# Rotated group order, sums of x beside the first expert, combinations on GpSimd and later stores in a fused sparse-attention and Sinkhorn-MoE kernel

## Chip, cores and metric

One core of a Trainium2 chip runs the whole program. The metric is device time in microseconds (us): the median over runs of the span that the device reports. TensorE does the matmuls (PE in the profile, PEld its weight loads), VectorE is DVE, ScalarE is ACT, GpSimd is POOL, and SyncE (SP) issues every DMA.

## The reference

```python
# attention: batch 4, heads 8, 576 positions, head size 64; masks local (32) or strided (32)
x = attention(q, k, v)                       # as rows: (2304, 512)
P = exp(x @ w_gate - max)                    # (2304, 8)
for _ in range(8):                           # Sinkhorn
    P /= P.sum(1, keepdims=True) + 1e-9
    P /= P.sum(0, keepdims=True) + 1e-9
    P *= N / E
out = 0
for e in range(8):                           # every expert, every row
    h = maximum(x @ w1[e], 0)                # 512 -> 1024
    out += P[:, e:e+1] * (h @ w2[e])         # 1024 -> 512
```

## The kernel before

Every matmul operand is split into a high and a low fp32r part, and a product is three matmuls (high times high, high times low, low times high).

**Attention and expert 0.** Attention comes first, then expert 0 runs in `slots`, each a `layer1` of one block of 128 hidden features for one chunk of rows and the `layer2` of the slot before it. The first half of the hidden features (36 slots, 256 rows each) runs beside the rest of the attention, the second half (20 slots, mostly 512 rows) beside gating and Sinkhorn. In the slots without attention work, Python generators are advanced a little per slot and so set the order of the instructions: `gating()`, and `build_s(p, k)`, which makes for row block p (of `NPASS` = 3, 768 rows each) and half k the four Strassen sums of x: it loads x from DRAM into the tile `sx`, adds two pairs on DVE (line 501), makes four sums on GpSimd (512), rounds them on ACT (518), subtracts on GpSimd (520) and stores the parts in DRAM (`sd`). Four of the six `build_s` run here, two beside pass 0.

**Experts 1 to 7.** Their work is cut into `NK` = 28 groups, an expert's quarter each (256 of the 1024 hidden features), and is done in three passes over blocks of 768 rows: `NG` = 84 groups. `step(g)` first ends the first layer of group g-1 (`finish_first`), then does the products of the first layer of g by Strassen's scheme (seven products of six matmuls each with 384 columns: 42 matmuls into the PSUM banks `ba`, `bb`, `bc`), then the second layer of g-1. In pass 0 the second layer is plain (`second`: 36 matmuls with 512 columns, line 676, each result added to `acc` on DVE, 683). In passes 1 and 2 it is Strassen's (`second_strassen`: 42 matmuls with 384 columns, 766, added to seven tiles `total` on DVE, 774), save in the last `LAST` = 2 groups of a pass, which are plain. After the last Strassen group of a pass, `combine` makes the result out of the seven totals (785: four operations on DVE, three on GpSimd, 128x768 each), and `turn` transposes it on TensorE and adds it to `acc` (794, 795), once per row tile, inside the loop of `second`.

**Weights.** In pass 0 `prep_w1` and `prep_w2` make the sums and the two parts of each group's weights out of the raw ones and store them in DRAM (`wd`, 598; `w2d`, 620); `w2_sums` forms its sums on DVE in two rows of `acc` (610 to 617). In passes 1 and 2 the same generators load them back (580, 632), group by group in the same order, into two buffers each (`g % 2`). The x operands of the next pass are loaded (`load_x`, 532 and 536) as the last group of a pass frees them one by one. `gated` multiplies by rows of the gate that `load_gate` broadcasts to all partitions (731), once per expert. In pass 0, after steps 4, 6, 8 and 10, `gate_rows` writes these rows (720, 721).

**Order.** All five engines work through their instructions in the order in which the program emits them; a wait at the head of a queue holds up all behind it. All DMAs are issued by SP, in order.

Of the kernel before, what the change touches and what calls it, by code (L numbers as in the profile page):

```python
# [55 lines left out]
def kernel(  # L56
# [429 lines left out]
    groups = [(p, e, j) for p in range(NPASS) for e in range(1, E) for j in range(FP)]  # L486
    NG = len(groups)
    wraw, w2raw, w2s, hg, yg, part = {}, {}, {}, {}, {}, {}

    def build_s(p, k):  # L490

        st = pools["sb"].tile([P, 4, 2, TN], F32, tag="sx", name=f"sx_{p}_{k}", bufs=1)
# [7 lines left out]
        for i in (0, 2):  # L500
            nc.vector.tensor_tensor(
                x[:, i : i + 2], x[:, i : i + 2], s[:, i : i + 2], op=ALU.add
            )
            yield
        x11, x21, x22, x12 = (x[:, i, :] for i in range(4))
        for i, (a, b, op) in enumerate((
            (x21, x22, ALU.add),
            (x21, x11, ALU.subtract),
            (s[:, 0, :], x11, ALU.subtract),
            (x12, s[:, 2, :], ALU.subtract),  # L510
        )):
            nc.gpsimd.tensor_tensor(s[:, i, :], a, b, op=op)
            if i % 2:
                yield
        yield
        for i in (0, 2):
            so = pools["sb"].tile([P, 2, 2, TN], F32R, tag="so", name=f"so_{p}_{k}_{i}", bufs=1)
            nc.scalar.activation(so[:, 0], s[:, i : i + 2], AF.Copy)
            yield
# [18 lines left out]
    def load_w1g(g):  # L538
        if g >= NK:
            return  # L540
        _, e, j = groups[g]
        if g == 0:
            t = raw_slots(4).rearrange("p (n i k f) -> p n i k f", n=4, i=2, k=2)
            wraw[g] = [t[:, i] for i in range(4)]
        elif g == 1:
            ts = [pools["hg"].tile([P, 2, TN], F32R, tag="hg", name=f"r_{g}_{i}") for i in range(4)]
            wraw[g] = [
                t.bitcast(F32).rearrange("p i t -> p (i t)")[:, : 4 * P]
                .rearrange("p (i k f) -> p i k f", i=2, k=2) for t in ts
            ]  # L550
# [15 lines left out]
    def load_w2g(g):  # L566
        if g >= NK:
            return
        _, e, j = groups[g]
# [4 lines left out]
    def prep_w1(g):  # L574
# [25 lines left out]

    w2o = [None, w2t.rearrange("p (b n) -> p b n", b=2)]
    w2sum = acc[:, HEAD : HEAD + 2, :].rearrange("p t d -> p (t d)")
    Q = 2 * P

    def w2_sums(g):

        src, w = w2raw.pop(g), w2o[g % 2]
        q = src.rearrange("p (n d) -> p n d", d=Q)
        t = w2sum.rearrange("p (n d) -> p n d", d=Q)
# [10 lines left out]
        nc.sync.dma_start(  # L620
            w2d[:, g, :].rearrange("p (b n) -> p b n", b=2), w.bitcast(F32)
        )
        yield

    def prep_w2(g):
        if g >= NG:
            return
        w = w2o[g % 2]
        if g >= NK:
            o = Q if strassen(g) else 0  # L630
            n = 8 * Q if strassen(g) else 4 * Q
            nc.sync.dma_start(
                w[:, :, o:n].bitcast(F32),
                w2d[:, g % NK, :].rearrange("p (b n) -> p b n", b=2)[:, :, o:n],
# [9 lines left out]
        if g:  # L644
            yield from w2_sums(g)
# [11 lines left out]
    LAST = 2  # L657

    def strassen(g):

        return NK <= g < NG and g % NK < NK - LAST

# [3 lines left out]
    def second(g, i, tag=None, parts=(0, 1)):  # L666

        p, e, j = groups[g]
# [17 lines left out]
        if ends(g):  # L686
            nc.sync.dma_start(out[t * P : (t + 1) * P, :], acc[:, i, :])

    def mul(g, wn, xn, bank, start):
        p, e, j = groups[g]  # L690
# [22 lines left out]
    gates, r11s = {}, {}  # L713
# [10 lines left out]
    def load_gate(p, e):  # L724
        if e == E:
            p, e = p + 1, 1
        if p == NPASS:
            return
        o = 2 * TN * (((E - 1) * (p - 1) + e - 1) % 2)
        t = raws[:, o : o + 2 * TN]  # L730
        nc.sync.dma_start(t, gd[e, 2 * TN * p : 2 * TN * (p + 1)].partition_broadcast(P))
        gates[p, e] = t.rearrange("p (h t) -> p h t", h=2)
# [6 lines left out]
    def gated(g, o, src, half):  # L739
        p, e, _ = groups[g]  # L740
        nc.vector.scalar_tensor_tensor(  # L741
            o, src[:, :TN], 0.0, gates[p, e][:, half, :], op0=ALU.max, op1=ALU.mult
# [33 lines left out]
    def combine():  # L776

        p1, p2, p3, p4, p5, p6, p7 = total
        for eng, o, a, b, op in (
            (nc.gpsimd, p2, p1, p2, ALU.add), (nc.vector, p6, p1, p6, ALU.add),  # L780
            (nc.vector, p7, p6, p7, ALU.add), (nc.vector, p6, p6, p5, ALU.add),
            (nc.vector, p3, p6, p3, ALU.add), (nc.gpsimd, p4, p7, p4, ALU.subtract),
            (nc.gpsimd, p5, p7, p5, ALU.add),
        ):
            eng.tensor_tensor(o, a, b, op=op)

    def turn(g, i):
# [7 lines left out]
        nc.vector.tensor_tensor(acc[:, i, :], y, acc[:, i, :], op=ALU.add)  # L795

# [31 lines left out]
    def step(g):  # L828
# [4 lines left out]
        if new:  # L833
            load_w1g(g + 2)
            if g >= NK:
                next(w2n, None)
                p, e, j = groups[g]
                if j == 1:
                    load_gate(p, e + 1)
# [26 lines left out]
        if new:  # L866
            mul(g, "t2", "s2", bb, True)
            plus(u2, bb, m1)
            next(w1n, None)
            mul(g, "t1", "s1", bc, True)  # L870
            next(w1n, None)
            next(w2n, None)
# [18 lines left out]
            if not strassen(g):  # L891
                relu_hi(g, 1, 1, u3)
        if not g:
            for x, only in rest:
# [6 lines left out]
        elif new:  # L901
            for i in range(6):
# [3 lines left out]
                if G >= NK and G % NK == NK - LAST:  # L906
                    turn(G, i)
                next(w1n, None)
                if i in (2, 4):
# [7 lines left out]
        for n in (w1n, w2n):  # L917
            for _ in n:
                pass
# [50 lines left out]
    def sums(*passes):  # L970
        for p in passes:
            for k in range(2):
                yield from build_s(p, k)

# [13 lines left out]
    def beside_second_half():  # L988

        work = {i: [] for i in range(20)}  # L990
        for g, i in enumerate((3, 12)):
            work[i].append(lambda g=g: load_w1g(g))
        for i, name in ((10, "x11"), (12, "s2"), (12, "s1"), (13, "x12")):
            work[i].append(lambda name=name: load_x(0, name))
        for g, s in enumerate((9, 15)):
            w = prep_w1(g)
            for i in range(5):
                work[s + i].append(lambda w=w: next(w, None))
        work[14].append(lambda: load_w2g(0))
        for i in range(6):  # L1000
            work[14 + i].append(lambda i=i: scale(0, i))
        return work

    slots = []
# [10 lines left out]
    for slot, (u, c, ft, last) in enumerate(slots):  # L1015
# [14 lines left out]
        if busy:  # L1030
            attention_rest()
            if at_k == NS + LAG:
                store_x()
                open_pools("right", ("sb", 1), ("hg", 8))
                gat, s0 = gating(), sums(0, 1)
                work = beside_second_half()
        else:
            next(gat, None)
            for _ in range(2):
                next(s0, None)  # L1040
# [3 lines left out]
    for x in (gat, s0):  # L1044
        assert next(x, x) is x
# [10 lines left out]
    s0 = sums(2)  # L1056
    for g in range(NG + 1):
        if g == NK:
            assert next(s0, s0) is s0
            open_pools("left", ("early", 2))  # L1060
        if g == NK + 1:
# [4 lines left out]
            ]  # L1066
        step(g)
        if g < NK:
            next(s0, None)
            if 4 <= g < 12 and g % 2 == 0:  # L1070
                gate_rows(g // 2 - 1)
            if g == NK - 1:
                load_gate(1, 1)
        p, n = divmod(g, NK)
        if 0 < p < NPASS:
            if n == 1:
                nc.sync.dma_start(
                    acc[:, :HEAD, :], yd[:, HEAD * (p - 1) : HEAD * p, :]
                )
            if 4 <= n < 4 + HEAD:  # L1080
                scale(p, n - 4)
# [81 lines left out]
```

## Time and profile before

| what | value |
|---|---|
| median of 3 runs | 1633.9 us (1633.17 to 6078.79) |
| profiled execution | 1634.83 us, its span 1633.0 us |
| PE busy | 1574.7 us, 96% |
| DVE / ACT / POOL busy | 1238.8 / 534.1 / 924.3 us |
| DMA | 426.26 MB, mean 261 GB/s |
| mean granted TensorE clock | 0.987 |

The span goes from the first to the last instruction. Matmuls are pipelined and the ends of their records are modelled, so starts are compared, not ends. A bracket at the end of a row of the timeline is the idle time of that engine ahead of the instruction and what ended it.

### The profile page before, as it was taken

To read this page: it belongs to the slowest core of one execution; us is meant where nothing else is said; L and a number is where in the kernel's file an instruction comes from. 1 tells how busy PE (TensorE), PEld (TensorE's weight loads), DVE (VectorE), ACT (ScalarE), POOL (GpSimd) and SP (SyncE) were. 2 spreads that over 40 slices of the span, in tenths; PEclk is the share of its full clock that TensorE was granted. 3 is DMA by queue.
4 is the path that set the end of the run, shared out by engine and by line. 5 is a ranking of instruction groups with operands and counts; after the bars stand their busy time and mean duration, and the time that the engine had idled before them with its cause. 6 is when DMAs were issued, how large, how long until landed. Compare 5 with 4: busy or idle time off the path is not lost.

```text
span 1633.0 us, 25381 instructions
## 1 busy us (share of the span) xinstructions
PE 1574.7 (96%) x9153; PEld 1467.9 (90%) x9153; DVE 1238.8 (76%) x2460; ACT 534.1 (33%) x1258; POOL 924.3 (57%) x880
## 2 busy tenths in 40 slices
PE   7999999989999999998999999999899999999997
PEld 5888778778888888887899999999899999999996
DVE  4665244389898989896488888888767888888886
ACT  6665222233434343432322222222223232222220
POOL 4221344146554656451577787777627778777781
PEclk9999999999999999999999999999999999999999
DMA  6553554697899789889966676666787666766661
GB/s 204 190 161 124 184 184 166 221 341 277 335 327 362 283 336 337 324 319 346 393 238 257 250 276 270 254 248 243 269 307 318 246 251 261 281 263 237 250 243 65
DMA packets 116700, 426.26 MB, mean 261 GB/s; under 512 B 9152, under 2 KB 62920, under 8 KB 101984
## 3 DMA queue, kind: packets, MB, share of 16 engines
q1 hardware_dynamic: 116576, 424.65, 69.5%
q8 instruction: 73, 1.20, 0.3%
q14 instruction: 51, 0.42, 0.1%
HBM read 287.72 MB, written 136.90 MB: 260 GB/s over the span
## 4 chain that ended last, share of the span: by engine, by line
PE 71%; DVE 16%; ACT 5%; DMA 4%; issue 2%; POOL 1%; SPq 0%; ACTq 0%; POOLq 0%; DVEq 0%
PE p L766 23%; PE bb L651 12%; PE ba L651 8%; PE bc L651 8%; PE yg L676 6%; PE y L429 5%; PE ph L405 5%; DVE acc L683 5%; DMA reg<-wd 2%; DVE acc L614 2%; DVE u L696 1%; ACT reg L180 1%; DMA sx<-xd 1%; DVE acc L613 1%; ACT h L704 1%
## 5 line engine op out<-in xcount | busy, mean ns | idle before, releaser
L774 DVE TENSOR_TENSOR total<-p,total 128x384 f32<-128x384 f32 x700 | 363.7, 557 | 0.0
L651 PE MATMUL bb<-reg 128*128 128x384 f32 x1512 | 310.4, 340 | 14.2 <-DVE u L696 8.9
L651 PEld LDWEIGHTS bb<-reg 128*128 128x128 f32 x1512 | 269.7, 190 | 19.3 <-DVE u L696 9.6
L651 PE MATMUL ba<-reg 128*128 128x384 f32 x1008 | 206.6, 340 | 11.3 <-ACT m L862 6.2
L651 PE MATMUL bc<-reg 128*128 128x384 f32 x1008 | 204.0, 336 | 6.8 <-ACT h L704 6.1
L651 PEld LDWEIGHTS ba<-reg 128*128 128x128 f32 x1008 | 181.6, 192 | 12.4 <-ACT m L862 6.5
L651 PEld LDWEIGHTS bc<-reg 128*128 128x128 f32 x1008 | 176.1, 188 | 13.0 <-ACT h L704 12.2
L696 DVE TENSOR_TENSOR u<-bb,m 128x384 f32<-128x384 f32 x168 | 93.2, 555 | 119.1 <-PE bb L651 117.4
L747 ACT ACTIVATE a<-u 128x384 fp32r<-128x384 f32 x104 | 54.7, 526 | 349.2 <-DVE u L741 349.0
L821 POOL TENSOR_TENSOR s1t<-m,u 128x384 f32<-128x384 f32 x52 | 52.9, 1016 | 187.5 <-DVE m L741 181.3
L683 DVE SCALAR_TENSOR_TENSOR acc<-yg,gate,acc 128x512 f32<-128x512 f32 x192 | 138.1, 743 | 12.6 <-PE yg L676 12.5
L429 PE MATMUL y<-w2t,h 128*128 128x512 f32 x432 | 112.3, 401 | 6.5 <-DVE h L412 5.6
L676 PE MATMUL yg<-w2t,h 128*128 128x512 f32 x504 | 117.7, 392 | 0.0
L676 PE MATMUL yg<-w2b,h 128*128 128x512 f32 x504 | 117.1, 390 | 0.0
L405 PE MATMUL ph<-reg,w 128*128 128x256 f32 (+1 forms) x672 | 114.3, 320 | 0.0
L676 PEld LDWEIGHTS yg<-w2t,h 128*128 128x128 f32 x504 | 95.0, 189 | 19.3
L766 PE MATMUL p<-s,w2t 128*128 128x384 f32 x624 | 112.3, 334 | 0.0
L766 PE MATMUL p<-s,w2b 128*128 128x384 f32 x624 | 112.3, 334 | 0.0
L676 PEld LDWEIGHTS yg<-w2b,h 128*128 128x128 f32 x504 | 94.4, 188 | 19.1
L766 PEld LDWEIGHTS p<-s,w2t 128*128 128x128 f32 x624 | 108.5, 188 | 0.0
L766 PEld LDWEIGHTS p<-s,w2b 128*128 128x128 f32 x624 | 108.5, 188 | 0.0
L751 POOL TENSOR_TENSOR a<-u,a 128x384 fp32r<-128x384 f32 x104 | 106.0, 1019 | 1.5 <-ACT a L747 1.5
(153 smaller groups left out, 2803.5 us busy)
## 6 DMA issues: line engine op xcount, KB each, us to landing
reg<-wd SPq DMA_DIRECT2D x56, 1792.0 KB, 10.0
wd<-reg SPq DMA_DIRECT2D x28, 1792.0 KB, 5.6
w2b<-w2d SPq DMA_DIRECT2D x26, 1792.0 KB, 6.8
w2t<-w2d SPq DMA_DIRECT2D x26, 1792.0 KB, 6.8
w2d<-w2b SPq DMA_DIRECT2D x14, 2048.0 KB, 7.6
w2d<-w2t SPq DMA_DIRECT2D x14, 2048.0 KB, 7.6
raws<-in_w SPq DMA_DIRECT2D x72, 256.0 KB, 4.8
sx<-xd SPq DMA_DIRECT2D x24, 384.0 KB, 5.6
```

Source lines behind the costliest of these rows:

```text
L405: nc.tensor.matmul(ph[:, :n], w[:, i, dt, :], xv(x, dt, c0, n), start=(k == 0), stop=(k == 3 * NDT - 1),)
L429: nc.tensor.matmul(y, h[:, a, i * P : (i + 1) * P], w[:, b, :], start=(ft == 0 and first), stop=(ft == FH - 1 and a == 1),)
L614: nc.vector.tensor_tensor(t[:, 3], t[:, 2], q[:, 3], op=ALU.subtract)
L651: nc.tensor.matmul(out[:, :TN], w[:, i, k, :], xops[x][:, xi, k, :], start=(start and n == 0), stop=(n == 5), skip_group_check=True,)
L676: nc.tensor.matmul(y, hg[g, i // 3, f][:, a, o : o + P], w[:, b, f, :], start=(f == 0 and a + b == 0), stop=(f == 1 and a == 1),)
L683: nc.vector.scalar_tensor_tensor(acc[:, i, :], y, gate[:, t, e : e + 1], acc[:, i, :], op0=ALU.mult, op1=ALU.add)
L696: nc.vector.tensor_tensor(o, bank[:, :TN], s, op=ALU.add)
L747: nc.scalar.activation(t[:, 0], src, AF.Copy)
L751: nc.gpsimd.tensor_tensor(t[:, 1], src, t[:, 0].bitcast(F32), op=ALU.subtract)
L766: nc.tensor.matmul(y[:, :TN], w[:, b, wi, d, :], h[:, a, :], start=(a + b == 0), stop=(a == 1),)
L774: nc.vector.tensor_tensor(o, y[:, :TN], o, op=ALU.add)
L821: nc.gpsimd.tensor_tensor(s1, m1, u3, op=ALU.add)
```

## The change

Groups carry a fourth number, their index k among the 28, and a pass begins with the two groups that the pass before ended with: pass 1 runs 26, 27, 0, ..., 25 and pass 2 runs 24, 25, 26, ..., 23. For these `KEEP` = 2 groups no weights are loaded. The store of the second-layer weights of groups 26 and 27 is put off until after steps 28 and 29. `LAST` becomes a tuple: pass 1 has one plain group at its end in place of two. The last part of `w2_sums` (617) and its store move from the end of a step into the next step, behind the second product; its sums get a tile of their own. In passes 1 and 2 the load of the second-layer weights is issued behind the products of a step, not at its head. All six `build_s` run beside expert 0, with two buffers for `sx` and a buffer for each `so`; their two additions go from DVE to GpSimd and their two subtractions from GpSimd to DVE. `combine` runs on GpSimd alone, and the six `turn`s stand behind the third to sixth block of `second`. The raw first-layer weights of group 1 use `raws`, those of the second layer of group 0 are loaded in the last slot instead of slot 14 of 20, and `acc` is loaded in six pieces.

```diff
-    groups = [(p, e, j) for p in range(NPASS) for e in range(1, E) for j in range(FP)]
+    KEEP = 2
+    groups = []
+    for p in range(NPASS):
+        for k in range(NK):
+            k = (k - KEEP * p) % NK
+            groups.append((p, 1 + k // FP, k % FP, k))
+    def kept(g):
+        return g >= NK and g % NK < KEEP
...
     def build_s(p, k):
-        st = pools["sb"].tile(..., tag="sx", bufs=1)
+        st = pools["sb"].tile(..., tag="sx", bufs=2)
...
-            nc.vector.tensor_tensor(
+            nc.gpsimd.tensor_tensor(
                 x[:, i : i + 2], x[:, i : i + 2], s[:, i : i + 2], op=ALU.add
             )
-            yield
...
+        for i, so in zip((0, 2), sos):
             nc.scalar.activation(so[:, 0], s[:, i : i + 2], AF.Copy)
-            yield
-            nc.gpsimd.tensor_tensor(
+        yield
+        for i, so in zip((0, 2), sos):
+            nc.vector.tensor_tensor(
                 so[:, 1], s[:, i : i + 2], so[:, 0].bitcast(F32), op=ALU.subtract
             )
...
     def prep_w1(g):
+        if kept(g):
+            return
         if g >= NK:
-            nc.sync.dma_start(whole, wd[:, g % NK, :])
+            nc.sync.dma_start(whole, wd[:, groups[g][3], :])
...
     def w2_sums(g):
+        w2sum = pools["hg"].tile([P, 2 * D], F32, tag="w2sum", bufs=1)
...
+        if g < NK - KEEP:
+            store()
+        else:
+            put_off.append(store)
...
     def prep_w2(g):
+        if kept(g):
+            return
...
-    LAST = 2
+    LAST = (NK, 1, 2)
+    def turning(g):
+        return g >= NK and g % NK == NK - LAST[groups[g][0]]
...
     def combine():
-        for eng, o, a, b, op in (
+        for o, a, b, op in (
+            (p6, p1, p6, ALU.add), (p7, p6, p7, ALU.add), (p6, p6, p5, ALU.add),
+            (p3, p6, p3, ALU.add), (p2, p1, p2, ALU.add), (p4, p7, p4, ALU.subtract),
+            (p5, p7, p5, ALU.add),
         ):
-            eng.tensor_tensor(o, a, b, op=op)
+            nc.gpsimd.tensor_tensor(o, a, b, op=op)
...
     def step(g):
-            if g >= NK:
-                next(w2n, None)
-        if g == 1:
-            for _ in w2_sums(0):
-                pass
...
             plus(u2, bb, m1)
+            for _ in w2_left.pop(G, ()):
+                pass
...
+        if g >= NK:
+            next(w2n, None)
         if not g:
+            for _ in range(3):
+                next(w2n, None)
             for x, only in rest:
                 layer2(*x, only)
...
-                if G >= NK and G % NK == NK - LAST:
-                    turn(G, i)
+                if turning(G):
+                    for x in ((), (), (0,), (1,), (2,), (3, 4, 5))[i]:
+                        turn(G, x)
...
+        if g < NK:
+            w2_left[g] = w2n
...
+    def beside():
+        for n in range(2 * NPASS):
+            w = build_s(*divmod(n, 2))
+            for i in (0, 3, 4, 5, 6):
+                at(3 * n + i - 4, next, w, None)
+        for g, i, s in ((0, 4, 9), (1, 14, 15)):
+            at(i, load_w1g, g)
...
+        at(19, load_w2g, 0)
```

## Rows read from the trace of the kernel before

**Rows 1.** The page, busy time of TensorE: us, share, instructions.
```profile
PE 1574.7 (96%) x9153; PEld 1467.9 (90%) x9153; DVE 1238.8 (76%) x2460; ACT 534.1 (33%) x1258; POOL 924.3 (57%) x880
```

**Rows 2.** Timeline of TensorE, starts of second layers: start, us, engine, line, operation.
```profile
334.40 8.36 PE L676 MATMUL yg<-w2b,h 128*128 128x512 f32 x36
...
752.94 8.36 PE L676 MATMUL yg<-w2b,h 128*128 128x512 f32 x36
...
776.33 9.02 PE L676 MATMUL yg<-w2t,h 128*128 128x512 f32 x36
...
798.24 2.07 PE L766 MATMUL p<-a,w2b 128*128 128x384 f32 x11
...
1163.02 2.25 PE L766 MATMUL p<-a,w2t 128*128 128x384 f32 x12
...
1204.81 4.28 PE L676 MATMUL yg<-w2t,a 128*128 128x512 f32 x18
...
1220.32 3.37 PE L766 MATMUL p<-a,w2b 128*128 128x384 f32 x18
...
1585.26 2.24 PE L766 MATMUL p<-a,w2t 128*128 128x384 f32 x12
...
1607.63 1.55 PE L676 MATMUL yg<-w2b,a 128*128 128x512 f32 x6
```

**Rows 3.** Waits from 150 to 320 us: us in total, times, longest.
```profile
DVE sx L501 <- DMA sx<-xd: 16.3, 5, 6.7
...
PE y L429 <- DVE h L412: 5.6, 2, 3.5
```

**Rows 4.** Timeline of TensorE beside gating, twice the same eight matmuls.
```profile
176.46 3.61 PE L339 MATMUL pl<-reg,wgs 128*128 128x512 f32 x8
...
186.29 2.00 PE L339 MATMUL pl<-reg,wgs 128*128 128x512 f32 x8
```

**Rows 5.** The tile sx, GpSimd's sums: ns min/median/max.
```profile
L512 POOL TENSOR_TENSOR sx<-sx x24: 995/1017/1209, 175.9 to 554.7; 128x384 f32<-128x384 f32 x24
```

**Rows 6.** Timeline of step 1.
```profile
323.30 1.21 PE L651 MATMUL bc<-reg 128*128 128x384 f32 x6
...
327.59 0.69 DVE L610 TENSOR_TENSOR acc<-raws 128x512 f32<-128x512 f32 x1 [4.46 <-DMA yd<-acc]
...
330.72 2.29 PE L651 MATMUL ba<-reg 128*128 128x384 f32 x6 [6.21 <-ACT m L862]
```

**Rows 7.** Timeline of a late step of pass 0.
```profile
715.48 1.26 DVE L617 TENSOR_TENSOR w2b<-acc,w2b 128x1024 fp32r<-128x1024 f32 x1
...
718.48 1.28 PE L651 MATMUL bc<-reg 128*128 128x384 f32 x6
...
721.67 0.56 DVE L708 SCALAR_TENSOR_TENSOR h<-ba,h 128x384 fp32r<-128x384 f32 x1 [1.71 <-ACT h L704]
```

**Rows 8.** Line 614, DVE: ns min/median/max.
```profile
L614 DVE TENSOR_TENSOR acc<-acc,raws x28: 424/1396/1953, 328.8 to 759.1; 128x256 f32<-128x256 f32 x28
```

**Rows 9.** The chain that ended last, between passes 0 and 1: start, us, what.
```profile
751.05 14.41 DMA reg<-wd
768.01 23.26 DMA reg<-wd
```

**Rows 10.** Stretch 750 to 800: busy us of each engine, granted clock, DMA share, GB/s.
```profile
750.00:800.00 50.00, 40.97 (x185) 36.47 (x185) 25.63 (x40) 8.92 (x18) 11.42 (x12) 0.90 1.01 400
```

**Rows 11.** Timeline between passes 1 and 2.
```profile
1166.63 1.30 PE L766 MATMUL p<-a,w2t 128*128 128x384 f32 x6 [1.37 <-DVE total L774]
...
1175.84 5.41 DVE L785 TENSOR_TENSOR total<-total,total 128x768 f32<-128x768 f32 x4
...
1181.77 2.29 PE L651 MATMUL bb<-reg 128*128 128x384 f32 x6 [4.48 <-DVE u L696]
```

**Rows 12.** Line 785, GpSimd's part of combine: ns min/median/max.
```profile
L785 POOL TENSOR_TENSOR total<-total,total x6: 1846/2520/2573, 1168.9 to 1602.6; 128x768 f32<-128x768 f32 x6
```

**Rows 13.** Line 632, loads of second-layer weights, all 56.
```profile
DMA to landing us min/median/max: 4.8/6.8/12.4
```

More of the change, by code (lines that the diff above doesn't have):

```diff
@@ L540, in load_w1g @@
             return
-        _, e, j = groups[g]
-        if g == 0:
+        _, e, j, _ = groups[g]
+        if g < 2:
             t = raw_slots(4).rearrange("p (n i k f) -> p n i k f", n=4, i=2, k=2)
             wraw[g] = [t[:, i] for i in range(4)]
[L545 to L550, printed above, removed]
         else:
@@ L643, in prep_w2 @@
         yield
-        if g:
-            yield from w2_sums(g)
+        yield from w2_sums(g)
     def product(w, x, out, start):
@@ L685, in second, with store_out @@
         )
-        if ends(g):
-            nc.sync.dma_start(out[t * P : (t + 1) * P, :], acc[:, i, :])
+        if ends(g) and not turning(g):
+            store_out(p, i)
+    def store_out(p, i):
+        t = 6 * p + i
+        nc.sync.dma_start(out[t * P : (t + 1) * P, :], acc[:, i, :])
     def mul(g, wn, xn, bank, start):
-        p, e, j = groups[g]
+        p = groups[g][0]
         product(wops[g % 2][:, :, W_AT[wn]], xn, bank, start)
@@ L722, in gate_rows, with load_gate @@
         nc.sync.dma_start(gd[:, 4 * P * c : 4 * P * c + n * P], lt[:E, : n * P])
[L724 to L727, printed above, removed]
+    spans = []
+    for g in range(NK, NG):
+        if strassen(g) and (not strassen(g - 1) or groups[g][1] != groups[g - 1][1]):
+            spans.append(g)
+    def load_gate(n):
+        if n == len(spans):
             return
-        o = 2 * TN * (((E - 1) * (p - 1) + e - 1) % 2)
+        p, e, _, _ = groups[spans[n]]
+        o = 2 * TN * (n % 2)
         t = raws[:, o : o + 2 * TN]
         nc.sync.dma_start(t, gd[e, 2 * TN * p : 2 * TN * (p + 1)].partition_broadcast(P))
-        gates[p, e] = t.rearrange("p (h t) -> p h t", h=2)
+        gates[spans[n]] = t.rearrange("p (h t) -> p h t", h=2)
     def form_tile(g, name):
@@ L795, in turn @@
         nc.vector.tensor_tensor(acc[:, i, :], y, acc[:, i, :], op=ALU.add)
+        if ends(g):
+            store_out(groups[g][0], i)
     def finish_first(g, s):
@@ L916, in step @@
                 second(G, i)
-        for n in (w1n, w2n):
-            for _ in n:
-                pass
+        for _ in w1n:
+            pass
+        if g < NK:
+            w2_left[g] = w2n
+        else:
+            next(w2n, None)
     LAG = 3
@@ L968 @@
         )
[L970 to L973, printed above, removed]
     def open_pools(side, *names):
@@ L1033 @@
                 store_x()
-                open_pools("right", ("sb", 1), ("hg", 8))
-                gat, s0 = gating(), sums(0, 1)
-                work = beside_second_half()
+                open_pools("right", ("sb", 1))
+                gat, work = gating(), beside()
         else:
             next(gat, None)
-            for _ in range(2):
-                next(s0, None)
             for x in work.get(slot - len(slots) + 20, ()):
@@ L1043 @@
         prev = (u, c, ft, last)
-    for x in (gat, s0):
-        assert next(x, x) is x
+    assert next(gat, gat) is gat
     for name in ("s3", "x22", "s4"):
@@ L1066 @@
             ]
+        if g == NK - 1:
+            load_gate(0)
         step(g)
         if g < NK:
-            next(s0, None)
             if 4 <= g < 12 and g % 2 == 0:
                 gate_rows(g // 2 - 1)
-            if g == NK - 1:
-                load_gate(1, 1)
+        elif g < NK + KEEP:
+            for store in put_off[g - NK :: KEEP]:
+                store()
         p, n = divmod(g, NK)
         if 0 < p < NPASS:
[L1076 to L1081, printed above, removed]
+            i = n - 3
+            if 0 <= i < HEAD:
+                nc.sync.dma_start(acc[:, i, :], yd[:, HEAD * (p - 1) + i, :])
+            if 0 <= i - 2 < HEAD:
+                scale(p, i - 2)
     for x in stacks.values():
```

74 lines of the change are left out of this document (34 added, 40 removed).

## Prediction

> **What bounds the kernel now.** I read the page first: TensorE is busy for 96% of the span [rows 1], so only two things can give time, fewer columns or fewer holes. Then the timeline of TensorE alone, where the reader is to compare starts of second layers. Between 798.24 and 1163.02 there are 25 steps of passes 1 and 2, 14.59 us each; nothing but TensorE sets them, so 84 matmuls of 384 columns take 0.174 us apiece. A plain step without disturbance takes 15.51 us (1204.81 to 1220.32), which leaves (15.51 - 42 x 0.174) / 36 = 0.228 us for a matmul of 512 columns [rows 2]. With these two paces every other interval shows its holes:
> - pass 0, 334.40 to 752.94: 26 steps, 418.5 us, 16.10 each, so 15.3 us more than 26 x 15.51;
> - pass 0 to 1, 752.94 to 798.24: 45.3 us for two plain steps, 14.3 too many;
> - pass 1 to 2, 1163.02 to 1220.32: 57.3 us for one Strassen step and two plain ones (45.6), 11.7 too many;
> - the end, 1585.26 to 1607.63: 22.4 us for a Strassen step, 7.8 too many [rows 2].
>
> The views of waits and of the timeline then say what makes each hole; they are cited where I use them. The stretches without holes, some 730 us of passes 1 and 2, can't get faster.
>
> **The change part by part.** The sum is made against the profiled execution, whose span is 1633.0 us with 1.8 us around it (1634.8); the median of the runs is 0.9 us below that, so the same saving is taken off 1633.9.
>
> *A. Sums of x beside expert 0.* DVE waits 16.3 us for the loads of `sx`, because its addition stands at the head of its queue, and the rectifying operation that TensorE needs (412) stands behind it: TensorE waits 5.6 us for that [rows 3]. After the longer wait it also runs at the lower of its two clocks: the same eight matmuls take 3.61 us instead of 2.00 [rows 4]. Together 7.2 us. The additions go to GpSimd, on which TensorE waits for nothing here, so these holes go. New are two more `build_s`: on GpSimd each is two additions of 128x768 (1.85 us, the least of that size [rows 12]) and four sums of 1.02 [rows 5], 7.8 us; it comes once in three slots of 24 x 0.228 = 5.5 us, so GpSimd has 16.4 us for 7.8, and the weight splits fit in the rest. What can wait on it is ACT: its rounding of the sums stands ahead of the next rectification. It is emitted a slot later, the loads three slots earlier, and a rectification has nearly a slot of slack, so I take 0.5 us lost (0 to 3). **Gain 6.7 (4 to 9).** The upper end is above 7.2, since the clock is also low for what stands around those eight matmuls.
>
> *B. Step 1.* DVE waits 4.46 us for the DMA that empties the two rows of `acc` which `w2_sums` borrows; ACT's copy of m stands behind ACT's rounding of these sums, and TensorE waits 6.21 us [rows 6]. After 323.30 three products (18 matmuls, 3.1 us) were left, so the second layer could begin at 326.4 instead of 334.40 [rows 2, 6]: a hole of 8.0. With a tile of its own nothing waits for that DMA. In its place the sums of group 0 run in step 0, ahead of the additions of expert 0's last `layer2` on DVE: one operation of 1024 (1.26 [rows 7]), two of 256 (0.42 [rows 8]) and one of 512 (0.8 as an estimate, twice a 256), 2.9 us, part of it while DVE has nothing else. What is late next is the PSUM bank of the third product of step 1, by 1.3 us (0 to 2.9). **Gain 6.7 (5 to 8).**
>
> *C. The steps of pass 0.* Two causes. First, two `build_s` stand in these steps and crowd DVE and GpSimd; they go. Second, at the end of a step DVE does line 617 (1.26 us, after a wait for ACT) ahead of the operations that free a PSUM bank, and the third product starts late for it [rows 7]. The change moves 617 behind the addition of the second product, where DVE now sits idle for 1.71 us [rows 7], so it costs nothing if it fits, and its store passes SP later, behind the loads of raw weights instead of ahead of them. The cover is thin: an operation of DVE on two SBUF tiles beside GpSimd takes longer, 1.40 us in the median against 0.42 at the least for the same shape [rows 8], so 617 may take 2.2 us and spill 0.5 us. The spill delays the middle of the step, while its end has become 1.26 us emptier; I take 0.1 us a step (0 to 0.5), 2.6 in all. The four `gate_rows` stay; I leave their steps the mean excess of 0.6, 2.4 in all. 15.3 - 2.6 - 2.4: **gain 10.3 (5 to 13).**
>
> *D. Pass 0 to pass 1.* The chain goes through two loads of `wd` that take 14.41 and 23.26 us [rows 9], and between 750 and 800 us the DMA engines are full at 400 GB/s, 20 MB in all [rows 10]. Kept groups take away two loads of `wd` and two of `w2d` (1792 KB each from the code, 7.3 MB), and two stores of 2048 KB (4.2 MB) move behind steps 28 and 29. Some 8.5 MB stay, 5.5 of them x: seven loads of 768 KB, each with about a step from its issue to its use. At 400 GB/s the first five need 9.8 us, and the one asked for last of these is wanted some 12 us later. Residue 0.8 us (0 to 6). **Gain 13.5 (8 to 14.3).**
>
> *E. Pass 1 to pass 2.* In place of three steps with two plain ones come two Strassen steps and a plain one. The wait of 1.37 us behind the two low parts stays [rows 11]. The wait of 4.48 us goes: DVE is held for 5.41 us by `combine` while the product's bank waits for it [rows 11]. On GpSimd seven operations take 1.85 to 2.57 us each [rows 12], 13 to 18 us. Counted from the start of the last Strassen second layer, the fourth total is there at about 7 us, so the two results that the first three turns need at 7 + 5 x (1.85 to 2.57) = 16.3 to 19.9; TensorE comes to the first turn at 14.59 + 1.37 + 3 x 1.37 = 20.1. The other two are there at 20 to 25, and wanted at 25.7 with some 0.5 for each turn. Both just fit, and nothing else on GpSimd is in a hurry there. New: beside a GpSimd that never pauses, two operations of `finish_first` on two SBUF tiles (708) can each wait for the rest of one of its operations, 0 to 3.7 us together; the product's bank stands behind them. I take 2. The turns: of the 41.8 us from 1163.02 to 1204.81 [rows 2], 14.59 + 1.37 + 4.48 + 15.51 are named, 5.8 left for turns and low clock; the transposes alone, at a quarter of 0.228, are 1.4. I take 3. After: 14.59 + 15.96 + 15.51 + 3 + 2 = 51.1 against 57.3. **Gain 6.2 (3 to 8).**
>
> *F. The end.* The same `combine` before the last plain step: 22.4 becomes 14.59 + 1.37 + 2 = 18.0. **Gain 4.4 (2.5 to 6.4).** The turns stay.
>
> *Nothing:* the loads of `acc` in six pieces (steps 31 to 36; they are used 20 steps later), `load_gate` (a step ahead), the raw weights of group 1 (in `raws`, which the split of group 0 has left by then).
>
> The Trainium skill, page "SBUF — State Buffer", section "Who interferes with whom", says that a VectorE instruction with two SBUF inputs and a GpSimd instruction that reads SBUF exclude one another, and the later one is blocked until the other ends. It speaks against putting more on GpSimd beside such operations; by it alone, with every 617 and both 708s blocked for a whole operation, C would be about 5 and E and F 4.5 and 2.7, and the time 1595. The trace agrees that the same operation takes from 0.42 to 1.95 us [rows 8].
>
> **Sum.** 6.7 + 6.7 + 10.3 + 13.5 + 6.2 + 4.4 = 47.8 us, 1633.9 - 47.8 = **1586 us**. The low ends together give 27.5 (1606), the high ends 58.7 (1575).
>
> **Rivals.**
> 1. *DVE becomes the pace of pass 0.* If 617 is blocked in its new place, a step stays near 15.8 to 15.9 and C gives 3 instead of 10: 1594. For it: the spread of line 614 [rows 8]. Against: the end of the step loses the same 1.26 us.
> 2. *The transition stays with the DMA.* If the loads of x are the late ones, most of the 14.3 stays: 1599. For it: the engines at 400 GB/s [rows 10]. Against: more than half of these bytes go.
> 3. *GpSimd crowds expert 0.* If ACT waits 3 us for each of six sums, 18 us of A's gain turn round: 1604. Against: 7.8 us of work in 16.4.
> 4. *Slower: second-layer weights arrive late.* Their load is now issued behind the products, 42 x 0.174 = 7.3 us later, in 52 steps of passes 1 and 2, and must land within 14.59 us. Above that each microsecond costs 52; from 15.5 us on all of the gain is gone, at 16 us the time is 1633.9 - 48 + 73 = 1659. For it: it now follows directly on the load of `wd`, which took up to 23.26 us [rows 9]. Against: the 56 loads of this kind land after 4.8 to 12.4, 6.8 in the median [rows 13].
>
> That the change doesn't do what it says would be a kept group that waits for its buffer all the same, which is rival 2.
>
> **Chances and range.** Forecast 0.74, rival 1 0.12, rival 2 0.06, rival 3 0.05, rival 4 0.03. What a measurement tells from no change is about 2%, 33 us, so 1601. The forecast, rival 1 and half of rivals 2 and 3 lie below: faster 0.89, within 2% 0.08, slower 0.03. The range takes in the high ends and rivals 1 and 2: 1575 to 1604.
>
> **What would show it.** Right: no wait of TensorE for 412 beside expert 0; second layers of pass 0 15.5 to 15.6 us apart; none of 20 us or more at the two transitions; the first turn without a wait; 85% or more of the steps of passes 1 and 2 still at 14.59. Wrong: TensorE waits for `w2b` or `w2t` in passes 1 and 2, ACT waiting for `sx` beside expert 0, or steps of pass 0 above 15.8.

## The result, and the profile after

The changed kernel takes 1596.2 us (median) against 1633.5 us for the kernel before on the same chip: ratio 0.9773, 95% interval 0.9751 to 0.9795. One run of each kernel (2188.5 and 6078.8 us) fell in a much slower state; the medians take it in and the ratio leaves it out. The profiled execution has a span of 1594.2 us, 38.8 less than before; the forecast took off 47.8. The page, busy time of each engine, answers to [rows 1]:

```profile
PE 1558.7 (98%) x9159; PEld 1461.1 (92%) x9159; DVE 1273.4 (80%) x2460; ACT 539.5 (34%) x1261; POOL 972.9 (61%) x899
```

Of the 38.8 us, 16.0 were busy time of TensorE and 22.8 its idle time. As before, the starts of second layers on TensorE's timeline tell where the time went; they answer to [rows 2]. The first two rows are the gate's first product and the first step's first product, which bound the stretch beside expert 0.

```profile
162.92 2.00 PE L339 MATMUL pl<-reg,wgs 128*128 128x512 f32 x8
...
313.72 1.22 PE L667 MATMUL ba<-reg 128*128 128x384 f32 x6
...
335.00 8.37 PE L696 MATMUL yg<-w2b,h 128*128 128x512 f32 x36
...
739.68 8.36 PE L696 MATMUL yg<-w2b,h 128*128 128x512 f32 x36
...
755.22 8.36 PE L696 MATMUL yg<-w2t,h 128*128 128x512 f32 x36
...
770.76 3.35 PE L794 MATMUL p<-a,w2b 128*128 128x384 f32 x18
...
1135.91 3.28 PE L794 MATMUL p<-a,w2t 128*128 128x384 f32 x18
...
1150.48 2.24 PE L794 MATMUL p<-a,w2b 128*128 128x384 f32 x12
...
1168.22 4.29 PE L696 MATMUL yg<-w2t,a 128*128 128x512 f32 x18
...
1186.65 3.59 PE L794 MATMUL p<-a,w2b 128*128 128x384 f32 x18
...
1551.18 2.25 PE L794 MATMUL p<-a,w2t 128*128 128x384 f32 x12
...
1568.92 4.29 PE L696 MATMUL yg<-w2b,a 128*128 128x512 f32 x18
```

Set against the same marks of the kernel before (its gate began at 163.85, its step 0 at 307.41), each part has its measured gain. E runs over three steps on either side, from 1135.91 in the changed kernel:

| part | before | after | gain | forecast |
|---|---|---|---|---|
| A, gate to step 0 | 143.6 | 150.8 | **-7.2** | 6.7 (4 to 9) |
| B, step 0 to its second layer | 27.0 | 21.3 | 5.7 | 6.7 (5 to 8) |
| C, 26 steps of pass 0 | 418.5 | 404.7 | 13.9 | 10.3 (5 to 13) |
| D, pass 0 to 1 | 45.3 | 31.1 | 14.2 | 13.5 (8 to 14.3) |
| E, pass 1 to 2 | 57.3 | 50.7 | 6.6 | 6.2 (3 to 8) |
| F, the end | 22.4 | 17.7 | 4.6 | 4.4 (2.5 to 6.4) |

These sum to 37.8; 0.9 more came ahead of the gate. Five terms came out near their size, and A has the wrong sign: without it the sum is 45.0 against the 41.1 forecast for those five. So the question for the experiments was what happens beside expert 0.

The view of waits of the changed kernel, TensorE's over the whole run (us in total, times, longest), names little there:

```profile
PE y L429 <- DVE tail L442: 6.9, 1, 6.9
PE pc L376 <- DVE g L373: 4.8, 2, 3.7
...
PE p L794 <- DVE total L802: 2.8, 2, 1.4
PE bb L667 <- DVE u L720: 2.5, 2, 1.3
...
PE bb L667 <- DMA reg<-sd: 1.6, 1, 1.6
```

The two waits of [rows 3] for the sums are gone. In their place stand one of 6.9 us at 300 us and two of 1.1 and 3.7 us at 248 and 256 us. The windows show what comes with them (us, busy of each engine, granted clock, DMA share, GB/s):

```profile
240.00:270.00 30.00, 24.81 (x123) 21.04 (x122) 25.12 (x43) 6.27 (x12) 19.36 (x15) 0.89 0.61 199
270.00:290.00 20.00, 20.00 (x88) 16.09 (x87) 6.55 (x6) 4.29 (x7) 13.35 (x11) 1.00 1.03 391
290.00:310.00 20.00, 13.09 (x48) 10.35 (x47) 7.51 (x9) 7.68 (x13) 7.71 (x7) 0.83 0.62 226
```

In the first and third TensorE stands idle for 5.2 and 6.9 us, 12.1 in all between the two marks, and the granted clock falls to 0.89 and 0.83 of 2.4 GHz. The kernel before was idle for 7.2 us between the same marks and had one stretch at a lower clock (0.91, from 160 to 200 us). Of the 7.2 us that A lost, 4.9 are thus more idle time. The other 2.3 are the same matmuls taking longer, as the lower clock makes them: behind the wait at 300 us twelve of them take 5.33 us instead of 2.88.

**The hole at 300 us** is read backwards on the timeline (start, us, engine, line, operation, wait and releaser):

```profile
277.30 1.33 SPq L542 DMA_DIRECT2D reg<-sd  x2
278.68 2.70 SPq L534 DMA_DIRECT2D sd<-so  x2
281.48 0.60 SPq L546 DMA_DIRECT2D reg<-xd  x1
282.12 4.46 SPq L534 DMA_DIRECT2D sd<-so  x2
286.64 5.59 SPq L565 DMA_DIRECT2D raws<-in_w  x4
...
292.54 0.85 ACT L527 ACTIVATE so<-sx 128x768 fp32r<-128x768 f32 x1 [9.32 <-DMA sd<-so]
296.45 0.84 ACT L527 ACTIVATE so<-sx 128x768 fp32r<-128x768 f32 x1 [3.06 <-DMA sd<-so]
...
297.62 1.27 POOL L592 TENSOR_TENSOR raws<-raws 128x512 f32<-128x512 f32 x1 [11.72 <-DMA raws<-in_w]
...
298.94 0.69 DVE L412 SCALAR_TENSOR_TENSOR h<-ph,h 128x512 fp32r<-128x512 f32 x1 [15.00 <-ACT h L411]
...
299.55 2.48 DVE L442 TENSOR_TENSOR tail<-y,tail 128x512 f32<-128x512 f32 x4
```

TensorE's own timeline has the wait:

```profile
300.38 5.33 PE L429 MATMUL y<-w2t,h 128*128 128x512 f32 x12 [6.91 <-DVE tail L442]
```

ACT's last two roundings write into `so`, whose stores of the sums before were issued behind 768 KB loads of x operands; with the DMA engines full (1.03, 391 GB/s) the four stores issued there each take 12.7 us to land, against 2.7 in the median of all 24. Behind the roundings stands ACT's copy of `h`, behind that DVE's rectification (line 412, [rows 3]'s victim too), behind that in DVE's queue the addition 442, which frees the bank that TensorE waits for.

**The waits at 248 and 256 us** lie in the short slots of 256 rows, where the gate's chain on DVE (lines 368 to 380) must pass between two products. Timeline of DVE and GpSimd there and in a slot before it:

```profile
227.30 1.85 POOL L510 TENSOR_TENSOR sx<-sx 128x768 f32<-128x768 f32 x1 [2.12 <-DMA sx<-xd]
227.72 1.45 DVE L369 TENSOR_SCALAR g<-g 128x18 f32<-128x18 f32 x1
...
242.78 1.84 POOL L510 TENSOR_TENSOR sx<-sx 128x768 f32<-128x768 f32 x1 [8.56 <-DMA sx<-xd]
243.27 1.52 DVE L380 SCALAR_TENSOR_TENSOR gate<-gate,r 128x144 f32<-128x144 f32 x1
...
245.66 1.83 POOL L510 TENSOR_TENSOR sx<-sx 128x768 f32<-128x768 f32 x1 [1.04 <-DMA sx<-xd]
245.67 1.99 DVE L371 TENSOR_TENSOR gate<-gate,g 128x144 f32<-128x144 f32 x1
...
252.45 1.25 DVE L380 SCALAR_TENSOR_TENSOR gate<-gate,r 128x144 f32<-128x144 f32 x1
...
255.81 0.60 PE L376 MATMUL pc<-g,ones 128*128 128x8 f32 x2 [3.72 <-DVE g L373]
```

Each of the three DVE operations at 227, 243 and 245 us, 0.2 to 0.3 us by itself, ends 0.02 to 0.17 us after the GpSimd addition beside which it began (229.17 and 229.15, 244.79 and 244.62, 247.66 and 247.49). The Trainium skill, page "SBUF — State Buffer", section "Who interferes with whom", says that the two engines share a port pair that one instruction holds whole; these ends agree with it. Ahead of the longer wait, at 256 us, DVE's queue first holds its own subtraction, a rectification and two pairs of additions (248.02 to 252.11 us), and then line 380 takes 1.25 us, beside a GpSimd operation on raw weights.

The other steps' signs came as forecast: plain steps of pass 0 are 15.51 us apart, Strassen steps 14.57, the transition to pass 1 has no interval over 15.6 us, and the first turn at 1172 us starts without a wait.

### The profile page after: what moved, and what is told of

The parts are those of the page before. It is cut to its first block, busy times and chain, and to the rows that moved or that the text cites. A ratio compares the mean times of both kernels' runs of the same rounds, so it can differ in the third digit from the quotient of the medians.

```text
span 1594.2 us, 25449 instructions
## 1 busy us (share of the span) xinstructions
PE 1558.7 (98%) x9159; PEld 1461.1 (92%) x9159; DVE 1273.4 (80%) x2460; ACT 539.5 (34%) x1261; POOL 972.9 (61%) x899
## 4 chain that ended last, share of the span: by engine, by line
PE 91%; DVE 3%; DMA 2%; ACT 1%; issue 1%; SPq 1%; POOL 0%; DVEq 0%; ACTq 0%; POOLq 0%
PE p L794 24%; PE bb L667 16%; PE yg L696 16%; PE bc L667 11%; PE ba L667 11%; PE y L429 5%; PE ph L405 5%; DMA sd<-so 1%; PE tp L283 1%; PE pv L296 1%; ACT sm L259 1%; PE sc L240 1%; PE pl L339 1%; PE sc L223 1%; PE pv L310 0%
## 5 line engine op out<-in xcount | busy, mean ns | idle before, releaser
L802 DVE TENSOR_TENSOR total<-p,total 128x384 f32<-128x384 f32 x714 | 371.1, 557 | 0.0
L667 PE MATMUL bb<-reg 128*128 128x384 f32 x1512 | 304.8, 336 | 4.5 <-DVE u L720 2.5
L667 PEld LDWEIGHTS bb<-reg 128*128 128x128 f32 x1512 | 265.6, 188 | 7.9 <-DVE u L720 3.1
L667 PE MATMUL ba<-reg 128*128 128x384 f32 x1008 | 201.9, 334 | 0.6 <-DVE u L720 0.6
L667 PEld LDWEIGHTS ba<-reg 128*128 128x128 f32 x1008 | 177.2, 188 | 1.0 <-DVE m L769 0.9
L703 DVE SCALAR_TENSOR_TENSOR acc<-yg,gate,acc 128x512 f32<-128x512 f32 x186 | 131.6, 742 | 13.0 <-PE yg L696 13.0
L794 PE MATMUL p<-s,w2b 128*128 128x384 f32 x648 | 116.7, 334 | 0.0
L794 PEld LDWEIGHTS p<-s,w2b 128*128 128x128 f32 x648 | 112.7, 188 | 0.0
## 6 DMA issues: line engine op xcount, KB each, us to landing
w2b<-w2d SPq DMA_DIRECT2D x25, 1792.0 KB, 10.6
w2t<-w2d SPq DMA_DIRECT2D x24, 1792.0 KB, 10.6
```

The source lines that it names most:

```text
L667: nc.tensor.matmul(out[:, :TN], w[:, i, k, :], xops[x][:, xi, k, :], start=(start and n == 0), stop=(n == 5), skip_group_check=True,)
L703: nc.vector.scalar_tensor_tensor(acc[:, i, :], y, gate[:, t, e : e + 1], acc[:, i, :], op0=ALU.mult, op1=ALU.add)
L794: nc.tensor.matmul(y[:, :TN], w[:, b, wi, d, :], h[:, a, :], start=(a + b == 0), stop=(a == 1),)
L802: nc.vector.tensor_tensor(o, y[:, :TN], o, op=ALU.add)
```

## The experiments

All ratios are to the kernel before, run beside each; the changed kernel itself is 0.9773. "Mark" is the start of the first second layer, 334.4 before and 335.0 after. First, four kernels on the hole beside expert 0.

**Three buffers for the roundings.**

```diff
- pools["sb"].tile([P, 2, 2, TN], F32R, tag=f"so{i}", name=f"so_{p}_{k}_{i}", bufs=1)
+ pools["sb"].tile([P, 2, 2, TN], F32R, tag="so", name=f"so_{p}_{k}_{i}", bufs=3)
```

> Theory 1 (a late store holds ACT, and with it the rectification, in the last slots of expert 0): three buffers for the rounded sums take away only the wait for the second store of the previous sums; the raw weights of group 1 still land at about 297 us and their rounding stands next on ACT, so the wait of 6.9 us shrinks by 0 to 3 us: 1593 to 1596 us. Theory 2 (the single buffer alone is the cause): the whole wait and the low clock behind it go, 9 us: 1587. Theory 3 (the sheer volume of sums on GpSimd and ACT is the cause): no change, 1596.

1593.1 us, ratio 0.9763 (0.9746 to 0.9781), mark 332.1. The hole at 300 shrinks only from 6.9 to 5.5 us, the wait of 3.7 stays. The single buffer is where ACT waits, but with a third one the next thing in the same full queue, the raw weights of group 1, is late.

**The loads of x operands last.**

```diff
- for i, name in ((10, "x11"), (12, "s2"), (12, "s1"), (13, "x12")):
+ for i, name in ((15, "x11"), (16, "s2"), (17, "s1"), (18, "x12")):
```

> The four loads of x operands ahead of step 0 are issued in slots 15 to 18 instead of 10 to 13. Theory 1 (the DMA queue is full with 4 MB of x operands and weights when the stores of the sums and the raw weights of group 1 are asked for): both land some 8 us sooner, the wait of 6.9 us and the low clock behind it go: 1587 us (1585 to 1590). Theory 2 (the single buffer alone): a part at most, 1592 to 1596. Theory 3 (volume of sums): 1596. If the x operands themselves come late now, step 0 waits for them and the gain shrinks by up to 3 us.

1589.3 us, ratio 0.9739 (0.9722 to 0.9757), mark 328.1. The hole at 300 is gone altogether: it was these 3 MB ahead of the stores and raw weights. Part of it came back in step 0, where x12 is now the late one:

```profile
308.60 2.16 PE L667 MATMUL ba<-reg 128*128 128x384 f32 x6 [3.89 <-DMA reg<-xd]
311.76 2.26 PE L667 MATMUL bb<-reg 128*128 128x384 f32 x6 [0.99 <-DMA reg<-sd]
```

**The gate's chain begun earlier,** in slots that are not short.

```diff
+ if not busy and slot - len(slots) + 20 < -7:
+     next(gat, None)
```

> Gating and Sinkhorn begin three slots earlier, so that no iteration falls into the four slots of 256 rows. Theory 1 (in these short slots the chain of DVE between two Sinkhorn matmuls, lengthened by GpSimd's additions and by the subtractions now on DVE, is longer than the slot): TensorE's waits of 1.1 and 3.7 us for it and the low clock behind them go, 7 us: 1589. Theory 3 (the volume of sums holds DVE wherever Sinkhorn stands): the waits move to other slots, 1594 to 1598.

1593.8 us, ratio 0.9767 (0.9746 to 0.9788), mark 330.6. The waits in the short slots go, but new ones stand elsewhere: 1.9 us for the column sums at 219 us, where the chain now runs beside GpSimd's additions (line 369 takes 1.36 us there), and 0.6 us twice for ACT. The hole at 300 stays at 5.7 us. Most of the 7 us hoped for is not there.

**All three together.**

> Three buffers, the later x loads and the earlier Sinkhorn together. Theory 1: the gains add up, no wait of TensorE above 1 us beside expert 0 is left: 1579 us (1576 to 1583), some 17 us below the changed kernel. Theory 3: 1592 to 1596.

1591.0 us, ratio 0.9749 (0.9728 to 0.977), mark 330.5: no better than the late loads alone. The gains don't add: between the gate and step 0 TensorE is idle for 3.6 us in both, here in the waits of 1.6 and 1.9 us that the earlier gate brings, there in one at 254 us. And x12 costs 4.1 us in step 0, as it does there (3.9).

Then four kernels that each undo one part.

**No kept groups.**

```diff
- KEEP = 2
+ KEEP = 0
```

> The changed kernel with KEEP = 0: no rotation, all weights loaded, no store put off; everything else of the change stays. Theory 1 (kept weights are what frees the transition from pass 0 to 1): the DMA-bound wait comes back there, 10 to 14 us: 1606 to 1610 us. Rival (the later issue of the second-layer loads, or the x loads alone, decide the transition): the intervals of the transition stay near 15.5, 1596 to 1599.

1602.3 us, ratio 0.9811 (0.9796 to 0.9826). This lies between the two forecasts. The transition is 22.89 + 15.54 us instead of twice 15.54, with one long wait on TensorE's timeline:

```profile
755.84 2.29 PE L667 MATMUL ba<-reg 128*128 128x384 f32 x6 [4.60 <-DMA reg<-wd]
```

So keeping is worth 7.4 of the 14.2 us of D (the whole time rises by 6), and something else in the change the rest; the last run below looks for it.

**Combinations on VectorE and GpSimd as before.**

```diff
- for o, a, b, op in (
-     (p6, p1, p6, ALU.add), (p7, p6, p7, ALU.add), (p6, p6, p5, ALU.add),
...
-     nc.gpsimd.tensor_tensor(o, a, b, op=op)
+ for eng, o, a, b, op in (
+     (nc.gpsimd, p2, p1, p2, ALU.add), (nc.vector, p6, p1, p6, ALU.add),
...
+     eng.tensor_tensor(o, a, b, op=op)
```

> The changed kernel with combine split over DVE and GpSimd as before. Theory 1: DVE is held for 5.4 us again at both places, the wait of 4.5 us and some low clock come back in place of 1.25 us: 4 to 5.5 us each, 1604 to 1607. Rival (GpSimd alone is only as good, because the two low parts are blocked beside it): 1596 to 1599.

1607.8 us, ratio 0.984 (0.9823 to 0.9856). The step after each last Strassen layer takes 22.8 us instead of 17.7, twice, and the wait of [rows 11] is back:

```profile
1170.63 2.29 PE L667 MATMUL bb<-reg 128*128 128x384 f32 x6 [4.47 <-DVE u L720]
```

**The second-layer sums drained at the end of their own step.**

```diff
- if i == 2 and g < NK:
+ if i in (2, 4) and g < NK:
...
- w2_left[g] = w2n
+ for _ in w2n:
+     pass
```

> The changed kernel with the last part of the sums of the second-layer weights and its store back at the end of its own step. Theory 1 (that operation ahead of the additions that free a bank costs 0.26 us a step): steps of pass 0 15.76 us instead of 15.51, 26 of them, 6.5 us: 1602 to 1603. Rival (with the sums of x gone DVE has enough room): 1596.

1604.5 us, ratio 0.9825 (0.9806 to 0.9843). Steps of pass 0 are 15.76 us, those with `gate_rows` 16.2 to 16.5, against 15.51 and 15.7 to 15.95: 8 us. In its old place the splitting operation (617 of before) takes 1.26 us, in the new one 1.58 to 1.96 in the median and 2.34 at most, and yet the new place is free.

**The sums for pass 2 moved back into pass 0** (two of six `build_s`, one step of the generator for each step of the kernel, in a pool of their own with one `so`).

```diff
- for n in range(2 * NPASS):
+ for n in range(2 * NPASS - 2):
...
+ s2 = (x for k in range(2) for x in build_s(2, k))
...
+     next(s2, None)
```

> The changed kernel with the two sums of x for pass 2 back in pass 0 (steps 0 to 11, one step of the generator each), the other four beside expert 0 in their new form. Theory 1: expert 0 loses its wait of 6.9 us with the low clock behind it, since the last sums there are two pairs of slots earlier, 9 us; in pass 0 ten to twelve steps take 0.3 to 0.8 us more, 3 to 8 us: 1590 to 1596. Rival (the volume of sums beside expert 0 costs nothing, the transfers of x do): expert 0 keeps the wait, pass 0 pays as well, 1599 to 1604.

1600.3 us, ratio 0.9798 (0.9784 to 0.9813). Beside expert 0 the hole at 300 goes (mark 324.6, 10.4 us sooner), but pass 0 pays some 14 us where 3 to 8 were expected, most of it in two waits:

```profile
351.71 4.88 PE L708 MATMUL yg<-w2t,h 128*128 128x512 f32 x12 [5.93 <-DVE acc L715]
...
451.17 4.61 PE L708 MATMUL yg<-w2t,h 128*128 128x512 f32 x12 [2.90 <-DVE acc L715]
```

They come from GpSimd. Its sums of x (lines 510 and 520 of this run) stand ahead of its sums of the raw weights (604 to 608); ACT's rounding waits for those, DVE for ACT, and TensorE for DVE:

```profile
338.12 5.24 POOL L520 TENSOR_TENSOR sx<-sx 128x384 f32<-128x384 f32 x4
...
346.26 0.63 ACT L180 ACTIVATE reg<-ru 128x512 fp32r<-128x512 f32 x1 [8.78 <-POOL ru L608]
```

All six beside expert 0 is thus the better place by 4 us, in spite of the hole.

Last, four kernels for what these left open.

**The loads of x operands spread:** two earlier, two later, x12 two slots sooner than in the late version.

```diff
- for i, name in ((10, "x11"), (12, "s2"), (12, "s1"), (13, "x12")):
+ for i, name in ((8, "x11"), (9, "s2"), (15, "s1"), (16, "x12")):
```

> The four loads of x operands beside expert 0 are spread: x11 and s2 earlier (8 and 9 instead of 10 and 12), s1 and x12 later (15 and 16 instead of 12 and 13), so that neither the stores of the last sums nor the raw weights of group 1 stand behind them and x12 is still issued two slots sooner than in the run with all four late. Theory 1 (the queue of transfers around 277 to 282 us makes the late rounding, x12 issued last makes the wait in step 0): no wait of TensorE over 2 us between 290 and 335 us, neither the 6.9 us of the changed kernel nor the 3.9 us for x12; second layer of group 0 starts at 325 to 328 us instead of 335.0, time 1584 to 1588 us. Theory 2 (the hole moves with whichever transfers are put there: expert 0 has no free place for 2.75 MB): a wait of 3 us or more at another place before 335 us, time 1590 to 1597 us.

1589.2 us, ratio 0.9737 (0.9713 to 0.9761); the profiled execution has a span of 1584.6. Mark 325.5, 9.6 us sooner than in the changed kernel, and TensorE's longest wait between 290 and 335 us is 1.95 us, for an operand whose region expert 0 frees last. The same two windows as above, now without a hole at 300 and with the one at 250:

```profile
240.00:270.00 30.00, 25.23 (x124) 21.36 (x123) 24.63 (x43) 6.60 (x12) 20.47 (x15) 0.89 0.72 250
290.00:310.00 20.00, 18.48 (x86) 15.42 (x85) 9.25 (x12) 7.24 (x14) 6.30 (x6) 1.00 0.89 332
```

The mechanism is the first theory's; the median is 1 us above its bounds.

**Spread, with three buffers and the earlier gate.**

> As the run with the loads spread, and with three buffers for the sums' upper parts and three steps more of the gate drawn in the short slots. Theory 1 (separate causes, that add up once x12 is in time): 1580 to 1584 us, the waits of TensorE before step 0 under 5 us in sum. Theory 2 (the waits in the short slots only move): within 2 us of the run with the loads spread alone.

1588.5 us, ratio 0.9729 (0.9711 to 0.9747): the best median, beating both kernels, but the same as the spread loads alone. The waits in the short slots only move: 1.6 us for ACT at 214 us, 1.9 for the column sums at 219 us, then 3.35 for the sum s3 in step 0.

**GpSimd's part of the sums left out.** Its operations work on 8 columns of 384.

```diff
- x[:, i : i + 2], x[:, i : i + 2], s[:, i : i + 2], op=ALU.add
+ x[:, i : i + 2, :8], x[:, i : i + 2, :8], s[:, i : i + 2, :8], op=ALU.add
...
- nc.gpsimd.tensor_tensor(s[:, i, :], a, b, op=op)
+ nc.gpsimd.tensor_tensor(s[:, i, :8], a[:, :8], b[:, :8], op=op)
```

> GpSimd's two additions and four sums in each build of sums of x work on 8 of 384 columns, so nearly all of GpSimd's part in the sums is left out (the output is not the reference's); every transfer, every rounding and every store stays. Theory 1 (GpSimd running beside VectorE lengthens the gate's chain in the short slots): VectorE's operations on the whole gate fall from 1.5 to 2.0 us back to 0.2 to 0.5, TensorE's two waits for the column sums (1.1 and 3.7 us) vanish, attention's end to step 0 falls from 153.6 by 4 to 8 us; the wait near 300 us for the last rounding stays if the stores alone make it. Theory 2 (VectorE's own subtractions and its queue make them): these two waits stay over 3 us in sum and the stretch falls by less than 3 us. Theory 3 (GpSimd's sums, not the stores, are what the last rounding waits for): the wait of 6.9 us near 300 us goes too, and the time falls by 12 us or more.

1593.0 us, ratio 0.9757 (0.9734 to 0.9781). From the gate to step 0 it is 145.7 us, 5.1 less than in the changed kernel. Line 371 by its view (ns min/median/max), first the changed kernel, then this one:

```profile
L371 DVE TENSOR_TENSOR gate<-gate,g x8: 307/454/1991, 215.0 to 258.5; 128x144 f32<-128x144 f32 x8
```

```profile
L371 DVE TENSOR_TENSOR gate<-gate,g x8: 307/308/310, 215.2 to 255.8; 128x144 f32<-128x144 f32 x8
```

The waits for the column sums fall from 4.8 to 1.7 us; what is left has DVE's own subtraction and additions ahead of it. The wait at 300 us stays, at 5.9: GpSimd's work is not what the roundings wait for, the stores are.

**No kept groups, and the load of w2 first again.**

```diff
- KEEP = 2
+ KEEP = 0
...
+ if g >= NK:
+     next(w2n, None)
```

> No group is kept, as in the run without kept groups, and the load of w2 in passes 1 and 2 is issued at the start of its step again, ahead of that of the first-layer weights, as in the kernel before. Without kept groups the transition to pass 1 took 22.89 and 15.54 us, where the kernel before had 23.39 and 21.91. Theory 1 (the later issue of the w2 load gave the second interval its 6.4 us): the second interval goes back to 20 to 23 us and the time is 1607 to 1611 us. Theory 2 (the rest of the change gave it: the loads of acc in six pieces from the fourth step on instead of one block in the second, and the stores): intervals as without the edit, within 1 us, and the time 1601 to 1604 us. Plain steps of pass 1 and 2 at 14.57 us by both.

1608.2 us, ratio 0.9858 (0.9833 to 0.9883), 6 us above the run without kept groups. The time is the first theory's, but the place is not: the three intervals from step 26 on are 22.83, 15.54 and 21.29 us, against 22.89, 15.54 and 14.67. The second, which the first theory wanted back at 20 to 23, is unchanged; the new hole stands one interval later, outside D. The chain of waits shows a `wd` load on the path there, which is not the second one of [rows 9] but the one after it (start, us):

```profile
776.97 12.79 DMA reg<-wd
```

So of D, 7.4 us come from the kept groups. Issuing the load of w2 behind the products is worth 6.6 us where no group is kept, but behind D. What took D's second interval from 21.91 us to 15.54 no run isolates. A candidate stands on SP's timeline: in the kernel before, the 2048 KB store of second-layer weights is issued ahead of the `wd` load that comes late, and in this run behind it, since the change put the store into the next step. First the kernel before, then this run:

```profile
762.01 0.32 SPq L620 DMA_DIRECT2D w2d<-w2t  x1
...
768.01 6.12 SPq L580 DMA_DIRECT2D reg<-wd  x1
```

```profile
753.39 0.43 SPq L586 DMA_DIRECT2D reg<-wd  x1
...
759.23 0.32 SPq L630 DMA_DIRECT2D w2d<-w2t  x1
```

## Why the prediction came out as it did

The forecast was 10 us too low, and the total hides a term with the wrong sign. A came out 13.9 us worse than forecast, far outside its own range; by chance C brought 3.6 us more, and 0.9 came ahead of the gate, where nothing had been forecast. The other terms came out by their mechanisms, D only in part.

**A is the term that was mis-sized, and its sign with it.** The step went "so these holes go", which is right: no wait for `sx` on DVE, and none of TensorE for 412 from that cause. It then priced what was new at 0.5 us (0 to 3), by GpSimd's room: 7.8 us of work in 16.4. That room was there: ACT waited for GpSimd's sums three times, 6.2 us in all and not 18, and the wait at 300 us stays when that work is left out, so the third rival is wrong as well. (ACT waiting for `sx` had been named as a sign of being wrong; it came, and was not the cause.) But two things were not costed. One is the stores and raw weights that the two more `build_s` put into a DMA queue that a 3 MB burst of x operands had filled: the hole at 300 us, 6.9 us idle and 2.5 in the slower matmuls behind it; the late and the spread loads remove it. The other is DVE's own chain: the gate's operations were taken to cost what they cost alone, while each can wait for the rest of a GpSimd addition; leaving that work out gave 5.1 us back, 3.1 of them in the waits for the column sums. The prediction had used just this mechanism for 617 and 708 and not looked for it beside expert 0.

**B** was right in cause. The late bank cost 0.37 us and not 1.3, but 1.65 us for an operand of x whose region the last slot of expert 0 frees were not in the sum, so 5.7 and not 6.7.

**C** was too careful. A loss of 0.1 us a step was taken for 617 in its new place, and it is nothing: 15.51 us, as undisturbed. It does take longer there, as feared, but DVE's idle 1.71 us [rows 7] covered it; the undoing run costs 8 us. The steps with `gate_rows` have an excess of 0.2 to 0.4 us instead of 0.6. The first rival, DVE as the pace of pass 0, is wrong.

**D** was right in size, and in that there is luck. Its working gave the whole of it to the bytes that go with the kept groups; the runs give those 7.4 of the 14.2 us, with the rest of the change in place, and what gave the other half is open. It is not the order of two loads alone that the prediction named as its fourth rival, the slower one: with the old order back, D's second interval stays short, and the hole that comes stands behind it. As to that rival, the loads of second-layer weights do land later, 10.6 us in the median and 13.7 at most against 6.8 and 12.4 [rows 13], but within a step of 14.57 us, and no wait of TensorE names them. The second rival is wrong.

**E and F** were right by their steps. GpSimd's seven operations take 1.84 to 2.14 us each, at the low end of [rows 12]; the wait of 4.48 us is gone and that of 1.38 stays. The turns cost the 3 us taken for them (18.43 us for their step against 15.51, with no wait in it), but as work of TensorE: the transposes had been put at 1.4. The 2 us for `finish_first` were 1.23 and 2.19 us for two operations of 0.56, and TensorE waits for 1.25 of it:

```profile
1157.29 13.53 POOL L812 TENSOR_TENSOR total<-total,total 128x768 f32<-128x768 f32 x7 [0.99 <-DVE total L802]
...
1163.32 2.19 DVE L732 SCALAR_TENSOR_TENSOR a<-u,a 128x384 fp32r<-128x384 f32 x1
...
1166.03 1.31 PE L667 MATMUL bb<-reg 128*128 128x384 f32 x6 [1.25 <-DVE u L720]
```

One sum of the prediction is off: the chances that it counts as faster make 0.74 + 0.12 + 0.055, which is 0.915 and not 0.89.

Left open: what shortened D's second interval; how the 3.7 us at 256 us divide between DVE's own queue and its operations made longer by GpSimd; and why the median of the spread loads lies 4.6 us above its profiled span, where that of the changed kernel lies 2.0 above, so that it is no better than that of the late loads although its second layers begin 2.6 us sooner.

## What to carry to other kernels

Work that is moved under a long stage brings its stores and loads along; cost these by the queue's state at the place where they will stand, not by the engine's room. A store that frees a single buffer, issued behind a burst of large loads, turns into a wait of the engine that refills the buffer, and of everything in order behind it. When small operations on VectorE form a chain with a deadline, count for each the rest of a GpSimd operation that may run beside it.

## What the runs showed of the hardware that was not expected

A one-input operation of 18 columns (line 369) went from 0.18 to 1.45 us beside a GpSimd addition, as did those with two inputs, while the reductions of the same chain (368 and 373) kept their 0.30 and 0.43 us in every slot. A 6.9 us wait of TensorE was followed by twelve matmuls of 512 columns in 5.33 us instead of 2.88, so that hole cost a third more than its length. And a store of 384 KB took from 2.4 to 12.7 us to land within the same stage.
